# Reordered first loads in a fused attention and two-mixture kernel

## The chip, the cores and the metric

The kernel runs on one core of a Trainium2 chip. Its engines are TensorE (PE, matrix products; PEld is its weight load), VectorE (DVE), ScalarE (ACT), GpSimd (POOL) and SyncE (SP), which here only issues DMAs. The metric is the device time of one execution in microseconds (us), the median of several runs.

## The reference

```python
def _attn_ref(q, k, v):                      # (4, 8, 576, 64): batch, heads, sequence, head size
    q_d = q.reshape(B, H, Sd, 4, D).mean(axis=3)          # the same for k_d and v_d
    out_d = sm_attn(q_d, k_d, v_d)                        # softmax attention of 144 pooled places
    out_up = np.repeat(out_d, 4, axis=2)
    mask = np.abs(pos[:, None] - pos[None, :]) < 4        # band of 7 around each place
    scores = np.where(mask, scale * q @ k.T, -1e9)
    out_local = softmax(scores) @ v
    return out_up + out_local

x = attn_out.transpose(0, 2, 1, 3).reshape(2304, 512)
h = x @ w_in;  x = (h * np.cos(h)) @ w_out                # first mixture, 512 -> 2048 -> 512
xn = x / rms(x) * rms_g                                   # second mixture, 512 -> 1536 -> 512
g = xn @ w_gate;  return (g * sigmoid(g) * (xn @ w_val)) @ w_out2
```

## The kernel before, in words

Everything is one program. A planner (`Order`) writes the order of every engine's instructions ahead of the run: each piece of work is a generator that asks for an engine and a length, for an event, or for a place out of a pool, and the planner hands out turns by earliest start and due time. On the chip each engine then works through its list strictly in that order, and SP issues the DMAs in its own.

The work has three stages. In the first, batch 0 is attended. **Pooled attention**: q and k are loaded in six pieces (tiles `pq`, line 854), summed over four places (`sum4`, q on DVE, k on POOL), transposed (`trq`), multiplied (`sps`), passed through exp (tile `E`), transposed (`tra`) and multiplied with the pooled v (`avp`), which gives `od`. The pooled v come from tiles `v` (lines 475 and 478, 16 loads) and are summed on POOL into `vh` and `vhl` (lines 499 to 506). **Local attention** goes by five blocks `u` of 116 places: q and k of a block are two loads (tile `raw`, line 791), v is four small ones (tile `vb`, line 807, three buffers), then come transposes (`btr`), banded scores (`bs`, which need the band mask `bm`), maximum, exp and normalisation on DVE, ACT and POOL (tile `bE`), a transpose (`bat`), the product with v (`bav`), the sum with `od` on DVE (line 755) and the split into a high and a low part, `big`, on ACT and POOL (lines 768 and 770). The 256 tokens of x tile 0 are complete with the first 24 places of block 2.

The second stage is the first mixture: products `h` (line 1004), h cos h on ACT and DVE, products `y` (line 1070). Its 32 weight pieces (even ones of `w_in`, odd ones of `w_out`, 512 KB each, lines 286 and 288) arrive as 64-bit numbers and are converted in place by `w_conv`: two DVE instructions (lines 311 and 317), two of ACT (315 and 319) and a subtraction on POOL or DVE (line 322). The attention of batches 1 to 3 runs beside it (loads of `pq` at line 431, of `rqk` at 791). The third stage is the second mixture (products `gvp` and `o`).

Memory for the first loads comes out of the 31 places `wa` and `wb` that later hold weights. `start()` takes its places at once; the six of `pq` go into a pool `pqp`, three of which become the tiles `E2` of the blocks' exp, and the other three return when the third `E2` is taken. The list `LOADS` orders the rest of `start()`: "w" stands for weight pieces, "r" for blocks' q and k, "v" for the pooled v. `keep_warm` fills planned gaps of PE with products of the identity (`warm`, line 246) up to the planner's time `FT`.

Of the kernel before, what the change touches and what calls it, by code (L numbers as in the profile page):

```python
# [12 lines left out]
ACTF = mybir.ActivationFunctionType  # L13
# [24 lines left out]
LOADS = (("w", 4), ("r", 1), ("v", 0), ("r", 1), ("w", 4), ("r", 3))  # L38
# [153 lines left out]
def fused_kernel(ctx: ExitStack, tc, q, k, v, w_in, w_out, w_gate, w_val, w_out2, rms_g, mask, bmask, out):  # L192
    nc = tc.nc
    PE, ACT, DVE, POOL, SP = nc.tensor, nc.scalar, nc.vector, nc.gpsimd, nc.sync
    S_ = Order()
# [213 lines left out]
    def pq_first(w, c, t, qs, place):  # L409
# [4 lines left out]
        give("pqp", place)  # L414
# [210 lines left out]
    def block(b, u, raw, pools):  # L625
# [33 lines left out]
        else:  # L659
            if u % 2 == 0:  # L660
                pl = yield take("pqp")
# [173 lines left out]
    def start():  # L835
# [3 lines left out]
        for n in [("pq", w, c) for c in range(3) for w in range(2)] + [("qs", w) for w in range(2)] + [("E", hp) for hp in (1, 2, 3)] \  # L839
                + [("v4", hp) for hp in range(4)] + [("vhl", 0)] + [("raw", u) for u in range(5)]:  # L840
            pl[n] = yield take(PLACES)

# [6 lines left out]
        qs = [early(("qs", w), [128, 9, 64]) for w in range(2)]  # L849
        for c, (u0, n) in enumerate(UC):  # L850
            for w in range(2):
                t = early(("pq", w, c), [128, 4, 4, 64])
                yield "SP", max(0.48, 0.37 * n)
                SP.dma_start(t[:, :n], pq_src(0, w, u0, n))
                done(("pq", w, c))
                S_.add(pq_first(w, c, t, qs[w], pl["pq", w, c]), 0.0, S_.now())
        E = EP + [early(("E", hp), [72, 2, 3, 2, 64]) for hp in (1, 2, 3)]
        for hp in range(4):
            yield "POOL", 0.8
            POOL.memset(E[hp], 0.0)  # L860
        yield take("E")
        for hp in range(4):
            S_.add(pooled(0, hp, E[hp]), 0.0)
        vh0 = early(("vhl", 0), [128, 2, 3, 128])
        vh0 = VH + [vh0[:, 0], vh0[:, 1]]
        for x in vh0:
            yield "POOL", 0.5
            POOL.memset(x, 0.0)
        yield "SP", 0.96, (0, None)
# [3 lines left out]
        yield "ACT", 1.0  # L873

        for x, (d0, d1) in enumerate(((0, 3), (3, 3), (3, 10))):
            for s, d in enumerate((d0, d1)):
                pr = slice(64 * s, 64 * s + 64) if d0 != d1 else slice(0, 128)
                if d0 != d1 or s == 0:
                    ACT.activation(out=bm[pr, x], in_=bf[pr, 16 - d:80 - d], func=ACTF.Copy)
        done("mask")  # L880
# [22 lines left out]

        first = 0
        for what, n in LOADS:
# [3 lines left out]
            elif what == "w":  # L909
                yield from words(n)  # L910
            else:
# [927 lines left out]
```

## Time and profile before

| what | value |
|---|---|
| median of 3 runs | 985.36 us (984.74 to 2394.44) |
| profiled execution, its own time | 986.51 us |
| its span, first to last instruction | 984.7 us |
| mean granted clock of PE | 0.994 |
| PE busy | 954.6 us (97%) |
| DVE busy | 724.0 us (74%) |
| POOL busy | 268.5 us (27%) |
| DMA, loads and stores of the queue | 134.85 MB, 45.4% of 16 engines |

Busy shares are means over the three stages, so they say little about any one of them; what bounds the start is read from stretches of the span. A busy PE includes the `warm` products, which compute nothing.

### The profile page before, as it was taken

What the parts mean: (1) busy time and instruction counts of PE and PEld (TensorE: products, weight loads), DVE (VectorE), ACT (ScalarE), POOL (GpSimd) and SP (SyncE); (2) the same over time, 40 slices, a digit from 0 to 9 for tenths busy, and PEclk for the clock granted to TensorE, in tenths of its full rate; (3) what the DMA queues carried; (4) which work ended last, traced back from release to release, by engine and by line L of the source; (5) the groups of instructions that cost most, each with busy time, mean ns of one, the idle gap of its engine ahead of it and who ended that gap; (6) DMA issues with size and microseconds to landing.
All of it is one profiled execution on the core that took longest, in us unless ns stands there. A gap on an engine that the chain in (4) does not pass through costs nothing.

```text
span 984.7 us, 19115 instructions
## 1 busy us (share of the span) xinstructions
PE 954.6 (97%) x7102; PEld 881.4 (90%) x7102; DVE 724.0 (74%) x1460; ACT 542.8 (55%) x1090; POOL 268.5 (27%) x325
## 2 busy tenths in 40 slices
PE   7788899999999999999999999999999999999998
PEld 7787788888988888888888889999999999999998
DVE  3889976577767675666577599586666688999895
ACT  3657886577676964657566475242322334544442
POOL 3867675444345311000042252000000014300000
PEclk9999999899999999999999999999999999999999
DMA  8788633567675554544331311133222144454432
GB/s 245 211 234 252 179 116 118 140 204 185 201 220 153 173 168 137 167 153 165 124 129 65 107 43 49 49 105 93 75 81 70 57 146 131 137 169 137 143 119 76
DMA packets 160333, 136.07 MB, mean 138 GB/s; under 512 B 72176, under 2 KB 133744, under 8 KB 160240
## 3 DMA queue, kind: packets, MB, share of 16 engines
q1 hardware_dynamic: 160240, 134.85, 45.4%
q8 instruction: 56, 0.92, 0.4%
q14 instruction: 37, 0.30, 0.1%
HBM read 98.64 MB, written 36.18 MB: 137 GB/s over the span
## 4 chain that ended last, share of the span: by engine, by line
PE 83%; POOL 4%; DVE 3%; SPq 3%; issue 3%; DMA 2%; ACT 2%; DVEq 0%; POOLq 0%; ACTq 0%
PE gvp L1493 26%; PE y L1070 19%; PE h L1004 18%; PE o L1746 13%; PE bav L745 2%; PE btr L641 1%; SPq L475 1%; POOL wwa L322 1%; DMA v<-in_v 1%; SPq L807 1%; PE avp L589 1%; PE bs L684 1%; PE yt L1398 1%; PE bat L720 1%; SPq L478 1%
## 5 line engine op out<-in xcount | busy, mean ns | idle before, releaser
L1493 PE MATMUL gvp<-xc,wc 128*128 128x384 f32 x1296 | 231.7, 335 | 0.0
L1493 PEld LDWEIGHTS gvp<-xc,wc 128*128 128x128 f32 x1296 | 225.6, 188 | 0.3
L1564 DVE TENSOR_TENSOR tmp<-gvp,tmp 128x384 f32<-128x384 f32 x180 | 99.3, 553 | 54.6 <-PE gvp L1493 51.4
L1004 PE MATMUL h<-big,wwa 128*128 128x256 f32 (+1 forms) x756 | 126.1, 320 | 1.6 <-DVE t L1029 1.0
L1004 PEld LDWEIGHTS h<-big,wwa 128*128 128x128 f32 x756 | 109.4, 193 | 11.9 <-DVE t L1029 1.2
L1746 PE MATMUL o<-wo,wc 128*128 128x256 f32 x972 | 118.9, 280 | 0.0
L1746 PEld LDWEIGHTS o<-wo,wc 128*128 128x128 f32 x972 | 116.1, 190 | 0.0
L1070 PE MATMUL y<-wwa,big 128*128 128x512 f32 x432 | 109.6, 398 | 1.7 <-DVE big L1040 1.7
L1070 PEld LDWEIGHTS y<-wwa,big 128*128 128x128 f32 x432 | 78.9, 188 | 18.7 <-DVE big L1040 2.7
L1004 PE MATMUL h<-big,wwb 128*128 128x256 f32 (+1 forms) x504 | 85.2, 320 | 0.1
L1070 PE MATMUL y<-wwb,big 128*128 128x512 f32 x324 | 82.3, 399 | 2.3 <-POOL big L1040 2.3
L1024 DVE SCALAR_TENSOR_TENSOR t<-kk,h 128x512 f32<-128x512 int32 x72 | 49.0, 681 | 42.4 <-ACT kk L1022 42.1
L1004 PEld LDWEIGHTS h<-big,wwb 128*128 128x128 f32 x504 | 73.1, 193 | 7.7 <-issue 0.8
L1022 ACT ACTIVATE kk<-h 128x512 int32<-128x512 f32 x72 | 42.7, 593 | 58.4 <-PE h L1004 58.2
L1070 PEld LDWEIGHTS y<-wwb,big 128*128 128x128 f32 x324 | 59.0, 188 | 14.7 <-POOL big L1040 2.9
L1630 POOL TENSOR_TENSOR wt<-wo 128x256 f32<-128x256 f32 x10 | 9.9, 987 | 208.7 <-DVE wc L1349 183.3
L1029 DVE TENSOR_TENSOR t<-h,t 128x512 f32<-128x512 f32 x72 | 49.3, 685 | 18.1 <-ACT t L1027 17.6
L1555 ACT ACTIVATE tmp<-gvp 128x384 f32<-128x384 f32 x36 | 17.7, 492 | 75.9 <-PE gvp L1493 75.9
L1027 ACT ACTIVATE t<-t,cst 128x512 f32<-128x512 f32 x72 | 51.9, 722 | 13.2 <-DVE t L1024 12.7
L1038 ACT ACTIVATE big<-t 128x512 fp32r<-128x512 f32 x72 | 45.2, 629 | 25.0 <-DVE t L1029 23.6
L1689 ACT ACTIVATE wc<-ut 128x512 fp32r<-128x512 f32 (+1 forms) x60 | 34.3, 584 | 43.4 <-DVE ut L1675 27.2
L1040 DVE TENSOR_TENSOR big<-t,big 128x512 fp32r<-128x512 f32 x54 | 40.0, 741 | 16.5 <-ACT big L1038 16.2
(185 smaller groups left out, 1737.8 us busy)
## 6 DMA issues: line engine op xcount, KB each, us to landing
us<-tmp SPq DMA_DIRECT2D x72, 192.0 KB, 2.0
uf<-us SPq DMA_DIRECT2D x48, 256.0 KB, 2.9
rawwa<-in_moe_w_out SPq DMA_DIRECT2D x21, 512.0 KB, 4.5
wfs<-rawwa SPq DMA_DIRECT2D x36, 256.0 KB, 2.3
rawwa<-in_moe_w_gate SPq DMA_DIRECT2D x12, 512.0 KB, 4.0
rawwa<-in_moe_w_val SPq DMA_DIRECT2D x12, 512.0 KB, 4.4
wf<-wfs SPq DMA_DIRECT2D x12, 512.0 KB, 4.1
vb<-in_v SPq DMA_DIRECT2D x80, 64.0 KB, 2.7
```

Source lines behind the costliest of these rows:

```text
L1004: PE.matmul(h[:, w_ * ci:w_ * ci + w_], a[:, ksl], x_at(x, kk), start=m == 0, stop=m == 11)
L1022: ACT.activation(out=kk, in_=h, func=ACTF.Copy, scale=INV2PI, bias=0.25)
L1024: DVE.scalar_tensor_tensor(out=t, in0=kk, scalar=TWOPI, in1=h, op0=ALU.mult, op1=ALU.subtract)
L1027: ACT.activation(out=t, in_=t, func=ACTF.Sin, scale=-1.0, bias=cst[:, 0:1])
L1029: DVE.tensor_tensor(out=t, in0=h, in1=t, op=ALU.mult)
L1038: ACT.activation(out=gh, in_=t, func=ACTF.Copy)
L1040: (POOL if e == "POOL" else DVE).tensor_tensor(out=gl, in0=t, in1=gh, op=ALU.subtract)
L1070: PE.matmul(y[j][b], g[:, tsl], a, start=(first and ci == 0 and i == 0), stop=(last and c == 15 and i == 2))
L1493: PE.matmul(bank, w[:, a, kk], xc[:, x, b, kk], start=first and i == 0, stop=i == 5, skip_group_check=True)
L1564: DVE.tensor_tensor(out=half(o), in0=a, in1=half(b), op=ALU.add)
L1689: ACT.activation(out=o[:, 0], in_=src, func=ACTF.Copy)
L1746: PE.matmul(b[m][1][:, l], u[0][x][:, j, l], w[:, y, k], start=(p == 0 and l == 0 and i == 0), stop=(p == C3 - 1 and i == 2), skip_group_c ...
```

## The change

`LOADS` gets three new letters and `start()` is split so that they can stand anywhere: "m" makes the band mask's copies, "q" loads the six pieces of pooled q and k, "e" clears the tiles of the pooled attention. The new list loads the mask, then q and k of blocks 0 and 1, then the pooled q and k, two weight pieces instead of four, the pooled v, block 2, four weight pieces, and blocks 3 and 4. A place is taken for the first `E2` at the start (`e2p`), so that blocks 0 and 1 need not wait for a pooled place; of the six pooled places the first two that come free serve the other two `E2`, and the other four go back to the weights' pools at once.

```diff
-LOADS = (("w", 4), ("r", 1), ("v", 0), ("r", 1), ("w", 4), ("r", 3))
+FB = 1
+LOADS = (("m", 0), ("r", 2), ("q", 0), ("e", 0), ("w", 2), ("v", 0), ("r", 1), ("w", 4), ("r", 2))
@@ pq_first
-        give("pqp", place)
+        cnt["pqp"] = cnt.get("pqp", 0) + 1
+        give("pqp" if cnt["pqp"] < 4 - (FB > 0) else place[2], place)
@@ block
-                pl = yield take("pqp")
+                pl = yield take("pqp" if u or not FB else "e2p")
@@ start
-                + [("v4", hp) for hp in range(4)] + [("vhl", 0)] + [("raw", u) for u in range(5)]:
+                + [("v4", hp) for hp in range(4)] + [("vhl", 0)] + [("raw", u) for u in range(5)] + [("E2", 0)] * (FB > 0):
             pl[n] = yield take(PLACES)
+        if FB:
+            give("e2p", pl["E2", 0])
...
+        def sums(cs):
+            for c in cs:
+                u0, n = UC[c]
+                for w in range(2):
+                    t = early(("pq", w, c), [128, 4, 4, 64])
+                    yield "SP", max(0.48, 0.37 * n)
+                    SP.dma_start(t[:, :n], pq_src(0, w, u0, n))
+                    done(("pq", w, c))
+                    S_.add(pq_first(w, c, t, qs[w], pl["pq", w, c]), 0.0, S_.now())
...
+        def pool0():
+            for hp in range(4):
+                yield "POOL", 0.8
+                POOL.memset(E[hp], 0.0)
...
+            for x in vh0:
+                yield "POOL", 0.5
+                POOL.memset(x, 0.0)
...
+            elif what == "q":
+                yield from sums(range(3))
+            elif what == "m":
+                S_.add(masks(), -10.0)
+            elif what == "e":
+                S_.add(pool0(), -10.0)
...
-        yield wait(("E2", 2))
-        for _ in range(3):
-            p = yield take("pqp")
-            give(p[2], p)
```

The order of all engines through much of the first mixture is planned anew by this; PE's lists agree again in their last 180 of some 665 rows. Three places matter for the prediction. In the fences a number behind a tile's name tells tiles of one name apart; line numbers of the changed kernel are 1 or 2 higher for the same work, and its pooled loads stand at line 887.

**SP, the start of its queue.** First before: pooled q and k (`pq`), v of blocks 0 to 2 (`vb`), the mask (`bf`), four weight pieces (`rawwb`), block 0 (`raw0`).

```order
L854 DMA pq00_109<-in_q 128x1024
L807 DMA vb_98<-in_v 64x4x64 x4
L854 DMA pq10_111<-in_k 128x1024
L807 DMA vb_99<-in_v 64x4x64 x4
L854 DMA pq01_117<-in_q 128x1024
L807 DMA vb_100<-in_v 64x4x64 x4
L854 DMA pq11_140<-in_k 128x1024
L854 DMA pq02_167<-in_q 128x256
L854 DMA pq12_183<-in_k 128x256
L872 DMA bf_259<-band_mask 64x144 x2
L286 DMA rawwb2_267<-in_moe_w_in 128x4x256
L288 DMA rawwb3_281<-in_moe_w_out 128x1024
```

Now, from the queue's first load on:

```order
L856 DMA bf_107<-band_mask 64x144 x2
L809 DMA vb_98<-in_v 64x4x64 x4
L793 DMA raw0_116<-in_q 128x8x64
L809 DMA vb_99<-in_v 64x4x64 x4
L793 DMA raw0_116<-in_k 128x8x64
L809 DMA vb_100<-in_v 64x4x64 x4
L793 DMA raw1_132<-in_q 128x8x64
L793 DMA raw1_132<-in_k 128x8x64
L887 DMA pq00_168<-in_q 128x1024
L887 DMA pq10_171<-in_k 128x1024
L887 DMA pq01_186<-in_q 128x1024
L887 DMA pq11_216<-in_k 128x1024
```

Four loads of local q and k moved ahead of the pooled ones; two weight pieces fell from the stretch ahead of the pooled v, whose 16 loads follow in both.

**SP, behind the pooled v.** Before: block 1 stands first here, block 2 behind four weight pieces, blocks 3 and 4 behind the v of block 3 (`vb_98`).

```order
L286 DMA rawwb8_525<-in_moe_w_in 128x4x256
L288 DMA rawwb9_573<-in_moe_w_out 128x1024
L791 DMA raw2_576<-in_q 128x8x64
L431 DMA pq_599<-in_q 128x512
L791 DMA raw2_576<-in_k 128x8x64
L431 DMA pq_625<-in_q 128x512
L807 DMA vb_98<-in_v 64x4x64 x4
L791 DMA raw3_624<-in_q 128x8x64
L791 DMA raw3_624<-in_k 128x8x64
```

Now, from block 2 on:

```order
L793 DMA raw2_433<-in_q 128x8x64
L793 DMA raw2_433<-in_k 128x8x64
L287 DMA rawwb5_446<-in_moe_w_in 128x4x256
L289 DMA rawwb6_473<-in_moe_w_out 128x1024
L287 DMA rawwb7_506<-in_moe_w_in 128x4x256
L289 DMA rawwb8_533<-in_moe_w_out 128x1024
L793 DMA raw3_535<-in_q 128x8x64
L793 DMA raw3_535<-in_k 128x8x64
L793 DMA raw4_586<-in_q 128x8x64
L793 DMA raw4_586<-in_k 128x8x64
L932 DMA cst_86<-in_moe2_rms_g 128x4x1
L433 DMA pq_617<-in_q 128x512
```

Block 2 now comes straight behind the pooled v and blocks 3 and 4 ahead of the `vb` that waits; the seventh and eighth weight pieces (`rawwb8_525`, `rawwb9_573` before) stand behind that `vb` now, and from the ninth piece on the two queues have it at the same or nearly the same place.

**POOL, from the end of the pooled v's sums.** Before:

```order
L506 TENSOR_TENSOR vhl0_235<-v43_394 48x64
L322 TENSOR_TENSOR wwa12_441<-rawwb4_286,wwa12_441 128x512
L322 TENSOR_TENSOR wwa17_522<-rawwb6_460,wwa17_522 128x512
L322 TENSOR_TENSOR wwa13_502<-rawwb5_293,wwa13_502 128x512
L375 TENSOR_TENSOR pq_599<-pq_599 128x2x128
L770 TENSOR_TENSOR big_93<-bt_627,big_93 128x4x116
L377 TENSOR_TENSOR qs_598<-pq_599 128x128
L375 TENSOR_TENSOR pq_625<-pq_625 128x2x128
L322 TENSOR_TENSOR wwa14_560<-rawwb7_482,wwa14_560 128x512
L377 TENSOR_TENSOR qs_598<-pq_625 128x128
L770 TENSOR_TENSOR big_93<-bt_742,big_93 128x4x116
```

Now (`big_93` three times: blocks 0 and 1, then the 24 places of block 2 that complete x tile 0):

```order
L323 TENSOR_TENSOR wwa17_332<-rawwb4_289,wwa17_332 128x512
L323 TENSOR_TENSOR wwa2_513<-rawwb5_446,wwa2_513 128x512
L323 TENSOR_TENSOR wwa4_583<-rawwb7_506,wwa4_583 128x512
L323 TENSOR_TENSOR wwa3_545<-rawwb6_473,wwa3_545 128x512
L376 TENSOR_TENSOR pq_617<-pq_617 128x2x128
L772 TENSOR_TENSOR big_93<-bt_640,big_93 128x4x116
L378 TENSOR_TENSOR qs_616<-pq_617 128x128
L772 TENSOR_TENSOR big_93<-bt_664,big_93 128x4x116
L376 TENSOR_TENSOR pq_657<-pq_657 128x2x128
L378 TENSOR_TENSOR qs_616<-pq_657 128x128
L323 TENSOR_TENSOR wwa5_596<-rawwb8_533,wwa5_596 128x512
L772 TENSOR_TENSOR big_93<-bt_785,big_93 128x4x24
```

Block 1's part follows block 0's after one instruction instead of four, and block 2's after three more; before, seven stood between the second and the third.

Counted over whole lists: `warm` products fall from 112 to 82, but 24 of them stand behind the first `h` now, against 4. Ahead of the first h cos h step (`t<-kk,h`) DVE has 8 instructions of line 312 and 7 of line 318 in the changed kernel, against 12 and 10 of the same two conversion steps (lines 311 and 317) before.

## Rows read from the trace of the kernel before

**Rows 1.** The page, part 1: busy us (share of span) xinstructions.

```profile
PE 954.6 (97%) x7102; PEld 881.4 (90%) x7102; DVE 724.0 (74%) x1460; ACT 542.8 (55%) x1090; POOL 268.5 (27%) x325
```

**Rows 2.** Busy time by stretch: width, engines (xinstructions), PE clock, DMA share, GB/s.

```profile
0.00:60.00 60.00, 48.04 (x536) 44.29 (x537) 36.28 (x68) 32.06 (x91) 38.62 (x58) 1.00 0.82 220
60.00:100.00 40.00, 35.82 (x374) 31.48 (x374) 37.47 (x62) 28.17 (x51) 29.81 (x31) 1.00 0.86 255
100.00:130.00 30.00, 26.62 (x202) 23.04 (x201) 28.44 (x55) 26.73 (x54) 18.63 (x22) 0.94 0.59 169
150.00:598.00 448.00, 442.51 (x3264) 383.83 (x3263) 308.45 (x619) 293.46 (x566) 138.16 (x173) 0.99 0.47 145
```

**Rows 3.** Timeline of PE: start us, us, instruction, [idle before <-releaser].

```profile
46.02 1.14 PE L745 MATMUL bav<-bt,vb 64*64 64x58 f32 x32
47.10 2.27 PE L246 MATMUL warm<-ident 128*128 128x128 f32 x18
...
64.33 1.14 PE L745 MATMUL bav<-bt,vb 64*64 64x58 f32 x32
...
67.76 1.73 PE L1004 MATMUL h<-big,wwa 128*128 128x256 f32 x12
...
106.16 1.54 PE L534 MATMUL sps<-pqs 64*72 64x144 f32 x8 [2.66 <-DVE bst L704]
...
171.25 1.96 PE L745 MATMUL bav<-bt,vb 64*64 64x58 f32 x30 [1.64 <-DVE bt L755]
```

**Rows 4.** Timeline of POOL, pooled v to x tile 0.

```profile
20.42 0.78 POOL L868 MEMSET vh<- 128x384 f32 x2
...
27.12 0.73 POOL L499 TENSOR_TENSOR v<-v 128x256 f32<-128x256 f32 x1 [5.20 <-DMA v<-in_v]
...
45.16 4.08 POOL L322 TENSOR_TENSOR wwa<-rawwb,wwa 128x512 fp32r<-128x512 f32 x3
49.21 0.72 POOL L375 TENSOR_TENSOR pq<-pq 128x256 f32<-128x256 f32 x1
49.89 1.61 POOL L770 TENSOR_TENSOR big<-bt,big 128x464 fp32r<-128x464 f32 x1
...
67.27 0.58 POOL L770 TENSOR_TENSOR big<-bt,big 128x96 fp32r<-128x96 f32 x1 [0.27 <-ACT big L768]
```

**Rows 5.** Timeline of SP's DMA issues: start us, us.

```profile
18.52 4.16 SPq L475 DMA_DIRECT2D v<-in_v  x1
...
40.45 0.43 SPq L791 DMA_DIRECT2D raw<-in_k  x1
...
47.08 2.73 SPq L807 DMA_DIRECT2D vb<-in_v  x4
...
60.46 0.42 SPq L286 DMA_DIRECT2D rawwb<-in_moe_w_in  x1
```

**Rows 6.** Busy time by stretch again: small rows (4 to 12 us), weight pieces (16 to 20).

```profile
4.00:12.00 8.00, 6.27 (x36) 5.87 (x35) 2.47 (x2) 0.82 (x2) 1.99 (x2) 1.00 0.93 227
16.00:20.00 4.00, 3.41 (x28) 3.11 (x28) 0.14 (x1) 1.39 (x4) 4.00 (x8) 1.00 1.05 352
```

**Rows 7.** Waits of SP's queue, 0 to 80 us: total us, times, longest.

```profile
SPq L431 <- POOL qs L377: 4.9, 4, 1.7
```

**Rows 8.** Timeline of DVE: start us, us.

```profile
29.80 0.99 DVE L555 TENSOR_TENSOR E<-E,stat 72x288 f32<-72x288 f32 x2
...
44.23 0.68 DVE L317 SCALAR_TENSOR_TENSOR rawwb<-rawwb 128x512 int32<-128x512 int32 x1
...
45.16 0.41 DVE L311 TENSOR_SCALAR rawwb<-rawwb 128x512 int32<-128x512 int32 x1
...
47.27 1.31 DVE L755 TENSOR_TENSOR bt<-bav,od 64x464 f32<-64x464 f32 x2 [1.69 <-PE bav L745]
```

**Rows 9.** Busy time by stretch, the two at a lowered PE clock.

```profile
106.00:110.00 4.00, 3.84 (x20) 3.44 (x21) 4.00 (x9) 3.93 (x6) 1.75 (x3) 0.57 0.81 224
171.30:178.50 7.20, 7.20 (x57) 7.07 (x58) 2.53 (x4) 1.70 (x5) 5.67 (x8) 0.54 0.52 111
```

More of the change, by code (lines that the diff above doesn't have):

```diff
@@ L847, in load @@
             yield "SP", us
[L849 to L869, printed above, removed]
+        yield "SP", 0.96
         bf = wb.tile([128, 144], F32, tag=f"wb{NB - 1}", name="bf")
@@ L872, in start @@
             SP.dma_start(bf[64 * s:64 * s + 64], bmask[0:64])
[L873 to L880, printed above, removed]
+        qs = [early(("qs", w), [128, 9, 64]) for w in range(2)]
         def values0():
@@ L902, in raws, with masks @@
                 S_.add(block(0, u, (t[:, 0], t[:, 1]), (None, (pl["raw", u][2], pl["raw", u]))), blk_due(0, u))
+        def sums(cs):
[7 more added lines that the diff above has]
+                    S_.add(pq_first(w, c, t, qs[w], pl["pq", w, c]), 0.0, S_.now())
+        def masks():
+            yield "ACT", 1.0
+            for x, (d0, d1) in enumerate(((0, 3), (3, 3), (3, 10))):
+                for s, d in enumerate((d0, d1)):
+                    pr = slice(64 * s, 64 * s + 64) if d0 != d1 else slice(0, 128)
+                    if d0 != d1 or s == 0:
+                        ACT.activation(out=bm[pr, x], in_=bf[pr, 16 - d:80 - d], func=ACTF.Copy)
+            done("mask")
+        E = EP + [early(("E", hp), [72, 2, 3, 2, 64]) for hp in (1, 2, 3)]
+        vh0 = early(("vhl", 0), [128, 2, 3, 128])
+        vh0 = VH + [vh0[:, 0], vh0[:, 1]]
+        def pool0():
+            for hp in range(4):
+                yield "POOL", 0.8
+                POOL.memset(E[hp], 0.0)
+            yield take("E")
+            for hp in range(4):
+                S_.add(pooled(0, hp, E[hp]), 0.0)
+            for x in vh0:
+                yield "POOL", 0.5
+                POOL.memset(x, 0.0)
         first = 0
```

## The prediction, made before the changed kernel ran

> **What bounds the kernel now.** I read the page first, then the span by stretches, then the timelines of PE, POOL, SP and DVE up to the first product of the mixture, then the waits. The page says that PE is busy 97% of the span [rows 1]; the stretches say where that holds. From 150 to 598 us PE is busy 442.5 of 448 us, and from there to the end it runs on alone, so behind 150 us a saving counts only as far as PE can start its work sooner. Up to 60 us PE's 48.0 busy us are mostly the warming products. DVE is the engine to look at in between: 36.3 of the first 60 us, but 37.5 of the next 40 and 28.4 of the 30 after those, that is 65.9 of 70 us [rows 2]. So there are three regimes: a start limited by loads and by chains of small steps, a stretch from 60 to 130 us in which DVE is full with weight conversions, h cos h and attention, and a long rest in which PE is full.
>
> The first h starts at 67.76 us [rows 3]. The chain ahead of it: the pooled v arrive, POOL begins to sum them at 27.12 and has the last at 45.16 [rows 4]; the products bav of blocks 0 and 1 follow at 46.02 [rows 3]. Block 2, needed for x tile 0, comes late: its k is issued at 40.45, behind four weight pieces [rows 5], and its bav runs at 64.33, its low part on POOL at 67.27 [rows 3, 4]. SP stands still ahead of the v of block 3, which waits for the bav of block 0 and goes out at 47.08 [rows 5]; blocks 3 and 4 are queued behind it.
>
> **Part 1, bytes ahead of the pooled v.** Before: six pooled pieces (2304 KB), twelve vb (768), mask (72), four weight pieces (2048), block 0 (512): 5704 KB. Now two weight pieces less and one block more: 5192 KB. The rows of q, k and vb are 256 bytes long, and the stretch with most of them moved 227 GB/s at a busy share of 0.93, while the one with weight pieces moved 352 at a full share [rows 6]. Taking off 1024 KB at 352 saves 3.0 us, adding 512 KB at 227 costs 2.3: net -0.7; at one rate for both (255 GB/s, the mean from 60 to 100 us [rows 2]) it would be -2.0. I take -1. The 16 loads of v themselves are paced by SP's issue in both.
>
> The Trainium skill, "DMA: Bandwidth & Descriptors", section "Why small descriptors are slow (HBM only)", puts a 256-byte descriptor at 11 cycles where 8 carry data, 27% lost, which speaks against loading blocks first; rows 6 agree, 244 against 335 GB/s for a full share. By the page's loss at the 352 of the weight pieces the added block would cost 2.0 us and the term be -1.0, inside what I have.
>
> **Part 2, POOL's sums of v.** They took 18.0 us, from 27.12 to 45.16 [rows 4], with two weight subtractions among them; now one stands there (-1.4, a third of the 4.08 us for three), but three of the four clearings of vh come between the sums instead of before them (+1.2, each half of 0.78). So they end about -0.2 from the sums themselves and -1 from part 1 sooner: about 44.0. The pooled scores start later, since pooled q and k are behind four loads (1024 KB, 4.5 us at 227 GB/s), but the last of their exp tiles was normalised on DVE by 30.8 [rows 8], and the last vh was summed only at 45.16; that slack covers it. If it doesn't, up to 4.5 us come back here; that is an end of the range.
>
> **Part 3, block 2 and the first h.** Block 2's loads now come straight behind v, some 6 us sooner, and its scores no longer wait. Behind 44.0: bav of two blocks by 45.6, four additions of od at half of 1.31 each on DVE by 48.2, block 2's normalisation with one conversion between (four steps, which I estimate at the 0.68 of line 317: 2.7) by 50.9 [rows 8]; transpose, copy and bav of block 2, 0.7 + 0.6 + 1.1, by 53.3; two more additions, 54.6. POOL's own list is longer: four weight subtractions (4 x 1.36), the sum of pq (0.72), big of block 0 (1.61), qs (smaller than pq's sum, 0.5), big of block 1 (1.61), pq and qs (1.2), a subtraction (1.36), the 24 places (0.58): 13.0 us behind 44.0 gives 57.0 [rows 4]. So the first h moves from 67.8 to about 57, **-11 us**. Blocks 3 and 4 no longer stand behind the waiting vb.
>
> **Part 4, what comes back while DVE is full.** The 11 us reach the end only if DVE follows. It idled 23.7 us of the first 60 [rows 2]. Blocks 0 and 1 fill a part of it, but DVE now begins with block 0's scores, later than it did with the first pooled sum; I put its idle time up to the same point at 19 to 24 us, so it is 0 to 5 us ahead. Beside that, four first steps (0.41) and three second steps (0.68) of the conversions stand behind the first h cos h instead of ahead of it: 3.7 us that come sooner for h but are owed to the weights that follow [rows 8]. The weights also limit it: the ninth piece, issued at 60.46 before, has the same place in SP's list; now it goes behind vb of block 2, whose bav ends about 53.3, plus four issues (2.73 for four [rows 5]): some 57, 3 to 4 us sooner, not 11. DVE and the weights so agree on a lead of 3 to 6 us; of the 11 I give back **+5** (bounds 0 and +11).
>
> **Part 5, warming products.** Twenty more stand behind the first h. Nine (18 instructions) took 2.27 us, so one is 0.25 us [rows 3] and twenty are 5.0 if the gap for which each was planned is not there, nothing where it is. PE idled in the stretch 60 to 130 for 7.6 us [rows 2], which is a place for most of them; I take **+1**. The thirty fewer in all lie in front of the first h, where PE is not the bound: 0.
>
> **Part 6, places.** In the first 80 us the longest of the queue's waits is that of the pooled loads (line 431) for a ring place, 4.9 us [rows 7]; a weight load (line 286) that waits for a place isn't in that view. Giving four places back sooner, and holding one more for E2, is worth 0; at the most as much as those 4.9 us would shift.
>
> Sum: -11 + 5 + 1 = **-5 us** on the profiled execution's 986.51, or 981.5; the median was 985.36, 1.15 less, so I forecast a median of **980.4**.
>
> **Rivals.** *The whole shift reaches the end.* If DVE's order, with conversions put behind h cos h, keeps PE fed, PE is 11 us ahead for good: 975 to 974. For it: PE had only 7.6 us of idle from 60 to 130 [rows 2]. Against it: DVE's 65.9 of 70 us, and the ninth piece's 3 to 4 us.
>
> *Nothing is left.* PE starts h sooner, runs out of converted weights after the first three h groups (the seventh piece now stands behind the vb of block 3 that waits for bav, and stood ahead of it) and meets the old schedule at 100 us: 985. For it: DVE's total work is the same, and in this regime it alone sets the pace. Against it: DVE has idle time to gain.
>
> *Slower: PE starves and its clock falls.* The place is 60 to 130 us, behind the first h groups. PE's wait of 2.66 us ahead of 106.16 was followed by a stretch at 0.57 of the clock, that of 1.64 ahead of 171.25 by one at 0.54 [rows 3, 9]; the two stretches of 4.0 and 7.2 us cost about half of that at full clock, 1.7 and 3.3 us. PE would be started 11 us sooner into a stretch in which less weight is ready; each hole would cost about 2.2 us of idle time and 2.5 of slow clock, 4.7. With one such hole and the warming products at +1 the time is that of before; it decides from the second on: three of them (14), the warming products at full price (5) and the gain of part 1 to 4 (-6) give +13, 998; for 2% (1005) there would have to be five. The rule that the clock is one of two steps, full when PE has been busy and half after it has idled, is in the Trainium skill, "TensorE: Matmul & The Clock Gate", section "What's actually happening". By that rule the trace agrees: the granted values lie between 1.2 GHz and 2.4 GHz only because the stretches in rows 9 are cut a little wider.
>
> *The change doesn't do what it says:* v of the pooled attention, not block 2, holds everything, and if POOL is later by the 4.5 us of part 2 the first h moves by 6 only and the rest is eaten by part 4: 985, as with "nothing".
>
> **How the numbers follow.** Forecast (977 to 983) 0.45, the whole shift 0.18, nothing left (983.5 to 987, with the last rival) 0.21, slower 0.16. The range takes the forecast, most of the whole shift and nothing-left, and the first hole or two of the slower case: 972 to 992. A reordering of the whole plan adds a scatter of a few us that no row prices. Two per cent is 19.7 us, about what a measurement of this kernel can tell from no change: faster by it would need a shift of twice the 11 us, 0.03; slower by it five holes, 0.04; within it 0.93.
>
> **What would show it.** Right: first h near 57 us, the last sum of the pooled v on POOL near 44, DVE's idle time of the first 60 us at 19 or less with more than 95% busy from 57 to 120, PE's idle from 57 to 130 larger than the 7.6 us of 60 to 130 now, and the second mixture's first gvp some 5 us sooner. Wrong: first h later than 62 (part 2 or 3), or low-clock stretches beyond the two of before (the slower rival), or a PE that is full from 57 us on (the whole shift).

## The result and the profile after

The changed kernel takes 992.97 us (median of 6, 990.35 to 994.13), the kernel before 984.55 beside it: ratio 1.0083, 95% interval [1.0071, 1.0096]. That is 8.4 us slower: the time moved the other way from the forecast of 980.4 and lies 1 us above its range. One of the six executions of the kernel before took 2394.44 us; the ratio goes by fast executions alone and leaves it out. The profiled execution took 993.51 us (span 991.7, granted clock 0.984).

First the stretches of the changed kernel, in the columns of [rows 2]:

```profile
0.00:60.00 60.00, 40.83 (x451) 36.49 (x452) 41.00 (x75) 30.65 (x87) 36.02 (x56) 0.88 0.77 209
60.00:100.00 40.00, 38.06 (x395) 34.45 (x394) 33.07 (x55) 31.27 (x54) 27.07 (x27) 0.96 0.82 240
100.00:130.00 30.00, 25.49 (x205) 22.09 (x204) 24.39 (x41) 23.04 (x42) 21.38 (x20) 0.89 0.55 158
150.00:598.00 448.00, 441.58 (x3259) 381.33 (x3260) 303.08 (x596) 297.96 (x573) 143.66 (x184) 0.99 0.47 147
```

DVE, the third pair, is busier in the first 60 us (41.0, before 36.3), as forecast, but then no longer full: 57.5 of the 70 us from 60 to 130, where it had 65.9 [rows 2]. It is full just behind that, from 130 to 150 us, where the kernel before had it 14.0 us busy. First before, then changed:

```profile
130.00:150.00 20.00, 18.62 (x162) 16.07 (x161) 14.04 (x29) 16.53 (x31) 17.36 (x21) 1.00 0.40 125
```

```profile
130.00:150.00 20.00, 16.39 (x122) 14.38 (x121) 19.86 (x33) 15.31 (x30) 18.44 (x20) 1.00 0.48 152
```

PE's granted clock is below 1 in each of the first three stretches (0.88, 0.96 and 0.89).

PE around the first h, to be read beside [rows 3] (the name has moved to L1018):

```profile
47.30 2.08 PE L747 MATMUL bav<-bt,vb 64*64 64x58 f32 x64
...
58.09 1.08 PE L722 MATMUL bat<-ident,bE 128*128 128x128 f32 x4 [3.83 <-DVE bE L708]
...
60.81 1.97 PE L747 MATMUL bav<-bt,vb 64*64 64x58 f32 x32
...
65.10 1.68 PE L1018 MATMUL h<-big,wwa 128*128 128x256 f32 x12
```

The first h is at 65.10 us: 2.7 sooner than 67.76, not 11. POOL's first sum of pooled k is at 19.16, of pooled v at 28.59, and its last sum of v ends at 46.39 (beside [rows 4]):

```profile
19.16 1.27 POOL L376 TENSOR_TENSOR pq<-pq 128x512 f32<-128x512 f32 x1 [17.82 <-DMA pq<-in_k]
...
28.59 0.72 POOL L501 TENSOR_TENSOR v<-v 128x256 f32<-128x256 f32 x1 [0.51 <-DMA v<-in_v]
...
45.62 0.77 POOL L508 TENSOR_TENSOR vhl<-v 48x64 f32<-48x64 f32 x1
```

DVE between bav of blocks 0 and 1 and that of block 2 (beside [rows 8]; L312 and L318 are the first and second step of a weight conversion):

```profile
45.33 0.88 DVE L318 SCALAR_TENSOR_TENSOR rawwb<-rawwb 128x512 int32<-128x512 int32 x1 [0.41 <-ACT rawwb L316]
...
46.93 1.20 DVE L312 TENSOR_SCALAR rawwb<-rawwb 128x512 int32<-128x512 int32 x1
...
48.70 1.12 DVE L318 SCALAR_TENSOR_TENSOR rawwb<-rawwb 128x512 int32<-128x512 int32 x1
...
50.68 2.64 DVE L757 TENSOR_TENSOR bt<-bav,od 64x464 f32<-64x464 f32 x4
53.35 0.69 DVE L703 TENSOR_REDUCE bst<-bE 128x8 f32<-128x512 f32 x1
...
55.60 1.22 DVE L312 TENSOR_SCALAR rawwb<-rawwb 128x512 int32<-128x512 int32 x1
56.74 1.21 DVE L708 TENSOR_TENSOR bE<-bE,bst 128x512 f32<-128x512 f32 x1
...
62.81 1.31 DVE L757 TENSOR_TENSOR bt<-bav,od 64x464 f32<-64x464 f32 x2 [2.69 <-PE bav L747]
```

And SP's weight loads: the third piece, the seventh, the ninth and the twelfth (beside [rows 5], where the ninth is at 60.46):

```profile
35.28 0.79 SPq L287 DMA_DIRECT2D rawwb<-in_moe_w_in  x1
...
56.29 0.59 SPq L287 DMA_DIRECT2D rawwb<-in_moe_w_in  x1
...
65.31 0.60 SPq L287 DMA_DIRECT2D rawwb<-in_moe_w_in  x1
...
77.56 0.59 SPq L289 DMA_DIRECT2D rawwa<-in_moe_w_out  x1
```

Where the time went is read from two windows, first h to last `yt` of the first mixture, here of the kernel before, then of the changed one:

```profile
67.80:597.90 530.10, 517.15 (x3893) 448.64 (x3893) 381.45 (x745) 360.38 (x693) 197.81 (x238) 0.99 0.50 152
```

```profile
65.10:605.40 540.30, 522.77 (x3940) 453.58 (x3936) 384.97 (x742) 370.56 (x704) 211.97 (x250) 0.99 0.50 153
```

This stretch takes 10.2 us longer. PE's idle time grows from 12.95 to 17.53 us (+4.6), its busy time by 5.6, of which warming products are 5.2 (48 instructions for 6.5 us here, 10 for 1.3 before). With the first h 2.7 us sooner that is +7.5, against +7.0 in the span. Behind the last `yt` the two run alike (386.3 and 386.8 us).

What PE waits for in these windows is in the view of its waits (us in total, times, longest), before and changed, longest first:

```profile
PE sps L534 <- DVE bst L704: 2.7, 1, 2.7
PE y L1070 <- POOL big L1040: 2.3, 2, 1.2
PE y L1070 <- DVE big L1040: 1.7, 2, 1.2
PE bav L745 <- DVE bt L755: 1.6, 1, 1.6
```

```profile
PE bat L722 <- DVE pqs L399: 3.3, 1, 3.3
PE sps L536 <- ACT at L579: 3.2, 1, 3.2
PE y L1084 <- POOL big L1054: 3.1, 2, 2.6
PE y L1084 <- ACT big L1052: 1.6, 1, 1.6
PE bat L722 <- DVE bt L697: 1.2, 1, 1.2
```

Products of the attention that runs beside the mixture (`bat`, `sps`, `tra`, `bav` and the like) account for 9.5 of the 17.5 us, where they had 6.3 of 12.9; the rest is mostly `y` waiting for h cos h (`big`). No wait in either view is put down to the conversion of a weight piece.

### The profile page after: what moved, and what is told of

Read it like the earlier page. It is cut to its first block, busy times and chain, and to the rows that moved or that the text cites. A ratio compares the mean times of both kernels' runs of the same rounds, so it can differ in the third digit from the quotient of the medians.

```text
span 991.7 us, 18990 instructions
## 1 busy us (share of the span) xinstructions
PE 951.3 (96%) x7042; PEld 877.0 (88%) x7042; DVE 727.2 (73%) x1452; ACT 550.3 (55%) x1096; POOL 275.3 (28%) x331
## 4 chain that ended last, share of the span: by engine, by line
PE 82%; DVE 9%; DMA 3%; ACT 3%; SPq 1%; issue 1%; POOL 0%; DVEq 0%; ACTq 0%; POOLq 0%
PE gvp L1507 26%; PE y L1084 17%; PE h L1018 17%; PE o L1760 13%; PE bav L747 2%; PE btr L643 1%; PE avp L591 1%; PE sps L536 1%; PE bs L686 1%; DVE rawwa L312 1%; SPq L809 1%; PE bat L722 1%; DVE rawwa L318 1%; PE yt L1412 1%; PE tra L572 1%
## 5 line engine op out<-in xcount | busy, mean ns | idle before, releaser
L1018 PE MATMUL h<-big,wwa 128*128 128x256 f32 (+1 forms) x756 | 124.8, 316 | 1.1 <-DVE t L1043 1.1
L1018 PEld LDWEIGHTS h<-big,wwa 128*128 128x128 f32 x756 | 108.2, 190 | 11.6 <-DVE t L1043 1.4
L1084 PE MATMUL y<-wwb,big 128*128 128x512 f32 x324 | 84.5, 405 | 4.4 <-POOL big L1054 2.6
L1018 PE MATMUL h<-big,wwb 128*128 128x256 f32 (+1 forms) x504 | 85.4, 322 | 0.0
L1018 PEld LDWEIGHTS h<-big,wwb 128*128 128x128 f32 x504 | 74.0, 196 | 7.1 <-issue 0.9
L1084 PEld LDWEIGHTS y<-wwb,big 128*128 128x128 f32 x324 | 60.2, 192 | 17.7 <-POOL big L1054 3.1
L1054 POOL TENSOR_TENSOR big<-t,big 128x512 fp32r<-128x512 f32 x20 | 29.1, 1455 | 110.7 <-ACT big L1052 104.1
L1052 ACT ACTIVATE big<-t 128x512 fp32r<-128x512 f32 x72 | 45.1, 628 | 23.5 <-DVE t L1043 22.7
```

The costliest lines, as they stand in the source:

```text
L1018: PE.matmul(h[:, w_ * ci:w_ * ci + w_], a[:, ksl], x_at(x, kk), start=m == 0, stop=m == 11)
L1052: ACT.activation(out=gh, in_=t, func=ACTF.Copy)
L1054: (POOL if e == "POOL" else DVE).tensor_tensor(out=gl, in0=t, in1=gh, op=ALU.subtract)
L1084: PE.matmul(y[j][b], g[:, tsl], a, start=(first and ci == 0 and i == 0), stop=(last and c == 15 and i == 2))
```

## The experiments

Every kernel was timed beside the kernel before; ratios below are to that. Each profile is of one execution, which for some kernels is slower than their median (e1 997.73 us for 995.11, e6 1002.2 for 997.40). Four moments or sums of each profile are set beside the ratio: the first h, when SP sends the twelfth weight piece, when the subtraction of the 24th converted piece ends, and PE's idle time between the first h and the last `yt`.

| kernel | ratio [95%] | first h | 12th sent | 24th ready | PE idle |
|---|---|---|---|---|---|
| before | 1 | 67.8 | 63.8 | 130.7 | 12.9 |
| changed | 1.0083 [1.0071, 1.0096] | 65.1 | 77.6 | 140.2 | 17.5 |
| e1 | 1.0096 [1.0063, 1.0128] | 66.9 | 78.4 | 141.3 | 21.1 |
| e2 | 1.0174 [1.0150, 1.0198] | 67.4 | 73.6 | 147.2 | 18.0 |
| e3 | 1.0070 [1.0054, 1.0087] | 60.8 | 78.4 | 145.1 | 21.4 |
| e4 | 1.0007 [0.9991, 1.0023] | 71.1 | 63.1 | 131.1 | 13.0 |
| e5 | 1.0143 [1.0102, 1.0184] | 67.3 | 69.9 | 140.8 | 21.0 |
| e6 | 1.0110 [1.0072, 1.0149] | 70.5 | 71.3 | 145.2 | 22.7 |
| e7 | 1.0198 [1.0169, 1.0227] | 66.4 | 78.6 | 141.9 | 21.5 |
| e8 | 1.0081 [1.0056, 1.0107] | 70.6 | 64.5 | 128.8 | 16.0 |
| e9 | 1.0086 [1.0061, 1.0111] | 69.2 | 81.8 | 144.3 | 16.6 |
| e10 | 1.0221 [1.0204, 1.0239] | 75.8 | 87.0 | 154.7 | 23.8 |
| e11 | 1.0107 [1.0088, 1.0126] | 68.2 | 84.5 | 143.0 | 20.9 |
| e12 | 1.0139 [1.0124, 1.0154] | 66.0 | 85.0 | 145.3 | 18.7 |
| e13 | 1.0126 [1.0106, 1.0145] | 66.0 | 70.4 | 144.7 | 18.9 |
| e14 | 1.0081 [1.0061, 1.0102] | 66.7 | 70.9 | 141.6 | 14.5 |
| e15 | 1.0171 [1.0154, 1.0188] | 67.2 | 66.6 | 140.1 | 20.8 |
| e16 | 1.0171 [1.0148, 1.0194] | 60.6 | 71.1 | 142.3 | 23.3 |
| e17 | 1.0156 [1.0139, 1.0174] | 68.2 | 70.3 | 139.4 | 19.2 |
| e18 | 1.0138 [1.0109, 1.0167] | 60.6 | 64.0 | 136.9 | 22.3 |

**Which part: e4 and e12.** e4 has the old order of the loads with the new places, e12 the new loads without the places. e4 is not quite the places alone: it keeps the new code of `start()`, so the band mask is loaded first and SP's steps no longer come after POOL's clearing.

```diff
+LOADS = (("q",0),("e",0),("m",0),("w",4),("r",1),("v",0),("r",1),("w",4),("r",3))   # e4
-FB = 1
+FB = 0                                                                              # e12
```

> The changed kernel with the loads in their old order (pooled q and k, mask, four weight pieces, block 0, v, block 1, four pieces, three blocks), so of the change only the places that are given back sooner are left. If the order of the loads carries the loss: 983 to 987, first h at 67 to 68, 4 warming products behind it. If the places alone carry it (their use reorders the plan behind 60 us): 990 to 994. If any new plan scatters by several us whatever the loads: anything from 980 to 992, with the first h where it was.

> The changed kernel without its places (no place given back sooner, none held for E2), so the new loads alone. The old loads with the new places gave 984.9, so if the two parts are separate the new loads alone carry the loss: 990 to 996, 24th piece at 138 or later. If it takes both: 984 to 988.

e4: 984.91 us, no difference. e12: 999.14, above the 990 to 996 that was expected. So the places cost nothing with the old loads, and the loss came with the new ones. (With the new loads the kernel that has the places is 6 us faster, which is less than a new plan alone moves, e7 below.) That the order of the loads carries the loss is the nearest reading, but not shown by this pair: both are new plans too, and a new plan alone moved the time by 8.5 and 11.5 us (e7, e8). e4 also says something of the first h: it comes at 71.14, the latest but one of the table, and the kernel is as fast as before.

**The warming products: e1.**

```diff
-FT = 90
+FT = 55
```

> The changed kernel with warming products planned only up to 55 us: the 24 behind the first h are gone, the other instructions keep their order. Theory W (warming products planned into gaps that are not there push PE's work back): PE's 5.2 us of them behind the first h go, 988 us, PE's idle time behind the first h stays near 17.5 us. Theory I (they stand in gaps that are there anyway, since PE waits for DVE and the weights): the idle time grows by about 5 us in their place, 992 to 993. Theory C (they keep the clock up): the half-clock stretches behind 65 us, 13.6 us long in the changed kernel, get longer, 994 or more.

995.11 us, no faster. Theory W falls: the 48 instructions are gone, but in the profiled execution (997.73 us) PE's idle time behind the first h is 21.1 us instead of 17.5, and its busy time hardly falls:

```profile
66.90:609.70 542.80, 521.66 (x3896) 450.26 (x3889) 383.20 (x741) 370.20 (x704) 210.54 (x250) 0.98 0.50 152
```

Theory I has part of it and C the rest: stretches at half clock (1.2 of 2.4 GHz) behind the first h sum to 20.5 us instead of 13.7, and executions lie between 987.89 and 998.64. So most of the warming products stood in gaps that are there anyway: without them the gaps show as idle time and as more of the lower clock.

**The start: e3.** Pooled q and k ahead of the two blocks.

```diff
+LOADS = (("m",0),("q",0),("r",2),("e",0),("w",2),("v",0),("r",1),("w",4),("r",2))
```

> The changed kernel with the pooled q and k loaded ahead of the two blocks instead of behind them. Theory P: the pooled scores are back at their old time (first sps product near 21 instead of 29.8 us), POOL starts on the pooled v sooner, the first h comes at 58 to 61 instead of 65.1 us and the time falls by 4 to 7 us, 986 to 989. Theory L (weights 7 to 9 decide, wherever the first h is): first h sooner, but the time stays within 990 to 994, since the ninth piece still waits behind the v of blocks 3 and 4.

The first h comes at 60.76 us, 7 sooner than before, and the time is 992.42, not distinguishable from the changed kernel. Theory P was right about the first h and wrong about the time; L's number came out. A first h that is sooner does not make the kernel faster here.

**The planner's time: e9, e10, e11.** The old `start()` had a pause in it: its SP steps behind the pooled loads came after POOL's clearing in the same generator. In the new code the loads run on without it.

```diff
             else:
+                yield "SP", 0.0, (28.0, None)      # e9; e10: 33.0; e11: 31.0 with e3's LOADS
                 yield from values0()
```

> The changed kernel with one more line: the planner may not place the loads of the pooled v before 28 us of its own time (it placed them from 19.8 on; the chip sent them from 17.8 to 34.0). The order of the loads in the list stays, only what the planner orders around and behind them changes; by its own figures the first h is then at 60.6 instead of 52.3 us (65.1 on the chip in the changed kernel; 71.0 by its figures and 67.8 on the chip in the kernel before). Theory T (the new loading code took out the pause that had kept the planner's time behind the chip's, so every order behind it is made for loads that have not come yet): the 24th converted piece is ready by 135 instead of 140.2 us and the time falls to 982 to 989. Theory L without T (these loads in this order bring the weights late, whatever the planner thinks): 24th piece at 139 or later, 990 to 996.

> The same with 33 us: by the planner's figures the first h is at 68.2, nearly as in the kernel before. Theory T: like the run with 28 us or better, 982 to 988, 24th piece by 135. Theory L without T: 990 to 996. Theory R (any new plan falls some us either way): the two pauses differ by 5 us or more from each other.

> Pooled q and k ahead of the two blocks, which gave the soonest first h so far (60.8 us), and the pooled v not before 31 us of the planner's time. Theory T: first h at 60 to 63 and the pace of the kernel before behind it, 978 to 985. Theory L without T: 24th piece later than 138, 990 to 995, whatever the first h.

993.96, 1007.19 and 996.80 us: theory T falls, as it does by e4, which lacks the pause too and is as fast as before. Planning the pooled v later only made the pieces later (the 24th at 143.0 to 154.7). The two pauses of e9 and e10 differ by 13.2 us, more than the 5 that theory R asked for.

**Two pieces, from both sides: e2, e5, e6, e17, e18.** The old list sends eight pieces by 36.7 us, the new one six by 37.8 and the seventh at 56.29, behind the v that wait for bav.

```diff
+LOADS = (... ("w", 2), ("v", 0), ("r", 1), ("w", 6), ("r", 2))     # e2; e17 with NRAW = 7
+LOADS = (... ("w", 4), ("v", 0), ("r", 1), ("w", 4), ("r", 2))     # e5
+LOADS = (("w",4),("r",1),("v",0),("r",1),("w",2),("r",3))          # e6, in the kernel before
+LOADS = (e3's with ("w", 6)); NRAW = 7                             # e18
```

> The changed kernel with six weight pieces instead of four between block 2 and the last two blocks, so eight pieces stand ahead of the loads that wait for bav of blocks 0 and 1, as in the kernel before. Theory L (weights 7 to 9 come late and DVE's conversions behind them leave PE without work between 85 and 160 us): the ninth piece goes out near 58 instead of 65.3 us, PE's idle time behind the first h falls from 17.5 to 13 or less, 985 to 988. Theory P (the gain was lost ahead of the first h, in the pooled scores that came late): first h still near 65, time 991 to 994. Theory W: 31 warming products stand behind the first h, so 1 to 2 us more than the changed kernel, 994.

> The changed kernel with four weight pieces instead of two ahead of the pooled v: eight pieces ahead of the last two blocks, as in the kernel before, and 1024 KB more ahead of v. Theory L (the supply of converted weights sets PE's pace from 85 to 160 us; the twentieth converted piece is ready at 128.3 us in the changed kernel and at 116.8 in the kernel before): pieces 7 to 12 are sent sooner than the 56 to 78 us of the changed kernel, the twentieth is ready at 118 to 122 and the time falls to 985 to 989. If only the first h counts: v come about 3 us later, first h at 68, 995 or more. Rival R (each new plan falls anywhere within some us): no relation between the twentieth piece and the time.

> The kernel before with two weight pieces less in front of blocks 2 to 4 (two instead of four), everything else as it was: block 2's q and k go out sooner, the seventh and eighth piece stand behind the v that wait for bav, which is that part of the change alone. Theory L: the seventh to ninth piece go out 5 us or more later than the 35 to 60 us of the kernel before, the twentieth converted piece is ready 5 to 10 us later, and the time grows by 4 to 8 us, to 989 to 993, although block 2 is sooner. My forecast's mechanism (first h sooner is what counts): first h at 62 or sooner and 980 to 983. Rival R: anywhere, without relation to the twentieth piece.

> The changed kernel with six pieces instead of four between block 2 and the last two blocks, and seven instead of five pieces that may be loaded and not yet converted, so that all eight go out by 40 us, ahead of everything that waits for a product (in the run with six pieces and the old five the eighth went out at 55 us and the ninth at 69). Theory E (eight pieces early, converted while DVE is still idle, are what the old list has and each slower one lacks): the eighth piece is converted by 69 us, the twelfth by 88 and the 24th by 134; 984 to 990 us. Theory D (in the new order DVE spends that time on the blocks' and the pooled scores, so pieces sent early only lie there): eighth piece at 70 or earlier but the 24th at 139 or later, 991 to 1001.

> The same with pooled q and k ahead of the two blocks. Theory E: first h at 60 to 64 us, 24th piece by 134, 978 to 986. Theory D: 24th piece at 139 or later, 991 to 1001, whatever the first h.

e6 moves two pieces behind the blocks in the kernel before, and nothing else in the list; the rest is planned anew. It takes 997.40 us, outside what theory L gave for it (989 to 993). The seventh piece goes out at 52.65 (35.20 before), the 24th is ready 14.5 us later:

```profile
52.65 0.60 SPq L286 DMA_DIRECT2D rawwb<-in_moe_w_in  x1
...
142.58 1.32 POOL L322 TENSOR_TENSOR wwb<-rawwa,wwb 128x512 fp32r<-128x512 f32 x1
143.86 1.31 POOL L322 TENSOR_TENSOR wwa<-rawwa,wwa 128x512 fp32r<-128x512 f32 x1
```

(The 24th ends with the second of these, at 145.2; at 130.7 in the kernel before.) Block 2's bav did not gain by it either: first h at 70.5, not 62. So the forecast's first step, that sending block 2's loads sooner brings the first h sooner, falls here in a single edit.

From the changed side the repair failed each time. In e2 the eighth piece went out only at 55.0 and the ninth at 69.3, so it did not test what it was made for; its 1002.57 us lie above every range given for it. In e5 the twentieth converted piece was ready at 115.2 us, sooner than the 116.8 of the kernel before, and it took 999.05 us where theory L had 985 to 989. e17 sent eight pieces by 38.1 us, and yet the 24th was ready at 139.4 and the time was 999.56 us. e18 has everything that I had asked for, first h at 60.65 and sixteen pieces sent by 66.7 us,

```profile
60.65 2.52 PE L1018 MATMUL h<-big,wwa 128*128 128x256 f32 x19
```

```profile
66.65 2.00 SPq L289 DMA_DIRECT2D rawwa<-in_moe_w_out  x1
```

with DVE busy 66.2 of the 70 us from 60 to 130, and the 24th piece is still at 136.9, PE's idle time 22.3 us and the time 997.38. Theory E falls. D's numbers for the 24th piece and the time came out for e17 (its eighth piece was converted at 72.6 us, not by 70), and e18's 24th piece lies between the two.

**Sending 9 to 16 sooner: e13 to e16.** A condition in the planner puts pieces ahead of batch 1's loads.

```diff
         yield wait("late")
+        yield wait(("wl", 1, 13))       # set where piece 14's load is issued; e14: 15
         for b in range(1, B):
...
+                if (b, u) == (1, 0):    # in block_v; e15 with e5's LOADS, e16 with e3's
+                    yield wait(("wl", 1, 13))
                 x = yield take("vb")
```

> The changed kernel with one condition in the planner: the loads of batch 1's blocks (q, k and v) may not be put on the list before the fourteenth weight piece. So pieces 12 to 14 no longer stand behind loads that wait for products. Theory L: the twelfth piece goes out at 68 to 70 instead of 77.6 us, the 24th converted piece is ready by 135 instead of 140.2, and the mixture ends (last yt product) at 598 to 601 instead of 605.4; 985 to 989 us. Theory D (DVE is the limit; late pieces only follow from what it does first): pieces sent sooner wait longer for their first step on DVE, 24th piece at 138 or later, 991 to 997.

> The same up to the sixteenth piece. Theory L: as with fourteen or 1 to 2 us better, 984 to 988, unless batch 1's blocks then come late for x tile 2, which would show as PE waiting for big behind 130 us. Theory D: 991 to 997.

> Four pieces ahead of the pooled v (999.1 us without the condition) and pieces 9 to 14 ahead of batch 1's loads. Theory L: the twelfth piece goes out below 70 us, the 24th is ready by 135, 986 to 992, 7 us or more better than without the condition. Theory D: 996 to 1001, no relation.

> Pooled q and k ahead of the two blocks (first h at 60.8 us, 992.4 without the condition) and pieces 7 to 14 ahead of batch 1's loads. Theory L: the twelfth piece goes out at 66 to 70 instead of 78.4 us, 24th piece by 136, and since the first h is 7 us sooner than in the kernel before, 979 to 986. Theory D: 991 to 996.

996.63, 992.50, 1001.16 and 1001.96 us. The twelfth piece does go out at 66.6 to 71.1 us, and the 24th is ready at 140.1 to 144.7 all the same. Theory L in its simple form (send sooner, be ready sooner) falls; D's ranges held for e13 and e14, while e16 is 6 us above its range. e14 shows what takes its place: with sixteen pieces in front, DVE has less to do from 100 to 130 (18.8 us busy, 24.4 in the changed kernel), and the work of the blocks on it moves behind 130 (instructions that write `bst`, `bE` or `bt` and begin from 130 to 160 take 8.9 us, 4.1 in the changed kernel).

**Planning anew: e7 and e8.** The same loads, with another figure for a load's landing in the planner.

```diff
-    DMALAT = 2.0
+    DMALAT = 2.05
```

> The changed kernel with the planner's figure for a load's landing at 2.05 instead of 2.0 us: the first products of PE keep their order, buffers and places are given out differently, and what follows is planned anew with the same loads. Rival R (the 8 us are an accident of one plan): the time moves by 4 us or more, down to 985 or up to 1000. Theory L (it is in the first loads): 990 to 995, the twentieth piece again at 125 to 131 us.

> The kernel before with the same figure at 2.05 instead of 2.0 us, so a plan made anew with the old loads. Rival R: moves by 4 us or more, to 989 or above or 981 or below. Theory L: 982 to 988, twentieth piece ready at 114 to 120 us.

1004.45 and 992.86 us: 11.5 us more than the changed kernel, 8.5 more than the kernel before, for nothing that any row of the start would price. Rival R is right about the size. But the two lose in different places. In e8 the 24th piece is ready at 128.8, sooner than before, and the kernel is slower all the same; it loses between 400 and 500 us, where PE waits for `big`:

```profile
448.60 0.49 PE L1070 MATMUL y<-wwb,big 128*128 128x512 f32 x1 [1.68 <-ACT big L1038]
450.00 2.80 PE L1070 MATMUL y<-wwb,big 128*128 128x512 f32 x11 [0.91 <-POOL big L1040]
```

From 400 to 500 us PE is busy 95.16 us in e8 and 99.65 in the kernel before. e7 has the changed kernel's late pieces (141.9) and loses more on top.

## Why the prediction was wrong

**The sign's cause.** Two steps failed. Part 3 put the first h at 57 us and the gain at 11 us; the gain was 2.7. And the sum took a lead of the first h for a lead of PE's end, less 5 and 1 us (parts 4 and 5); behind the first h 10.2 us were lost. In the terms of the sum, forecast -11 + 5 + 1 = -5 against -2.7 + 10.2 = +7.5, part 3 was short by 8.3 us and parts 4 and 5 together by 4.2. The second step is the deeper one, for where part 3's aim was reached, in e3, e16 and e18 (first h at 60.6 to 60.8), the time was 992 to 1002 us, and e4, with the first h at 71.1, took 985. Over the twenty kernels of the table the first h says nothing of the profiled span (correlation 0.11). PE's idle time behind it (0.82) and the 24th converted piece (0.73) go with the span, but less so among the seventeen kernels that do not have the old loads (0.64 and 0.47), and PE's idle time is itself a part of the span.

The three kernels that have the old loads (before, e4, e8) have the 24th piece at 128.8 to 131.1, all seventeen others at 136.9 or later. An early 24th piece is a sign of the old loads, then, and not shown to be the cause of their time: e8 has the earliest and takes 992.86 us, and no weight piece stands in the two views of PE's waits above.

The forecast's own signs of being wrong came: the first h later than 62, and low-clock stretches beyond the two. The second mixture's first gvp, forecast some 5 us sooner, came at 584.4 us instead of 576.9, 7.5 later.

**Part 1** (-1 us): POOL's first sum of v is 1.5 us later, not sooner; SP began the sixteen v sooner but spread them further, from 17.77 to 33.38, where it had been 18.52 to 31.92. Bytes alone did not tell it.

**Part 2** (sums of v end at 44.0): 46.39. The slack for the pooled scores held, in the sense that POOL's last sum still ended behind DVE's last normalisation of E (43.8); but those normalisations now lie at 37.1 to 43.8, where conversions had stood.

**Part 3** (-11 us): from bav of blocks 0 and 1 (47.30) to that of block 2 (62.78) I had 44.5 to 53.3. DVE first did conversion steps and block 2's own scores, which I had taken as done, so the sums with `od` began at 50.68; block 2's normalisation took from 53.35 to 57.95, 4.6 us instead of four times 0.68, since single instructions were stretched to 1.21 and 1.22; and bat and bav ran at half clock, 1.08 and 1.97 us where they take 0.60 and 1.14 at 68.48 and 70.69. The POOL list that I thought longer was not what decided: ahead of the low part of the 24 places POOL idled 1.9 us for ACT.

**Part 4** (+5, bounds 0 and 11): the ninth piece, forecast at 57, was sent at 65.31, behind batch 1's v that wait for block 2's bav, and DVE was not over 95% busy from 57 to 120 us but 86% (54.1 of 63 us). Parts 4 and 5 together were 10.2 us, of a lead that was 2.7. That DVE and the supply of weights would set the lead is not what the runs show: DVE was less busy than before, and PE's waits were for the attention and for h cos h.

**Part 5** (+1, bounds 0 and 5): 5.2 us of PE's time, but without them e1 was no faster. **Part 6** (0): right with the old loads (e4).

**The rivals.** The slower one, at 0.16, named what came: holes for PE behind the first h and a falling clock. Idle time grew by 4.6 us, and half-clock stretches behind the first h by 3.4: there are three, of 6.8, 3.4 and 3.4 us at 117.5, 151.6 and 175.5, where there were two of 3.4 and 6.8 (rows 9 cuts them wider). Each begins within 1.2 us of the end of a wait of PE: 3.33 us up to 117.03, 3.21 up to 150.48, 1.60 up to 174.93. Its sum of +13 was for three more holes, and one half-clock stretch more came; its reason, that less weight is ready, is not in PE's waits.

```profile
117.50:124.30 6.80, 6.77 (x32) 5.81 (x31) 4.93 (x11) 5.60 (x12) 4.17 (x2) 0.50 0.21 76
```

Its place, 60 to 130, was somewhat too early: counted in PE's instructions other than the warming ones, the changed kernel is 3.0 us ahead at 84 us and 0.5 at 103, and 2.8 behind at 125 and 8.0 at 158.

**What stays open.** Shown is where the time went: idle time of PE behind the first h, more of it at half clock, and warming products in gaps. Shown too is that a sooner first h (e3), no warming products (e1), pieces sent sooner (e5 and e13 to e18) and a later plan for the pooled v (e9 to e11) do not bring the time back, and that the places cost nothing with the old loads (e4). That the order of the loads is the cause is likely, since no kernel with a changed order was under 992.4 us, but it is not shown: a plan made anew from the same loads lies 8.5 to 11.5 us higher (e7, e8), and e8, with the old loads, takes 992.86. So part or all of the 8.4 us may be no property of these loads, but of leaving one plan that was better than its neighbours; against that, e4's plan is new as well and cost nothing. Which move of the order would do it is open too. The one remark on "a scatter of a few us that no row prices" was too small by a factor of two to three, and should have widened the range upwards and taken chance from "faster". No experiment separates the two shares, and no version beat the kernel before.

## What to carry to other kernels

Where an engine's lists are written by a planner, price the change only after pricing a plan made anew without it: here that alone was 8.5 us with the old loads and 11.5 with the new, as much as the largest term of the sum. The first product of a stage is a poor goal when other engines feed the stage: list what the stage's own engine waits for behind that product (here the attention beside it and h cos h, and in neither profile a weight piece), and ask of each load that is moved ahead which loads now queue behind a wait. Warming products in gaps aren't cheap or dear by themselves; taking them out only showed the gaps.

## What the runs showed of the hardware

DVE's first conversion step takes 0.41 us alone [rows 8], but up to 3.33 us beside POOL. The case, DVE first, then POOL:

```profile
144.67 0.68 DVE L1043 TENSOR_TENSOR t<-h,t 128x512 f32<-128x512 f32 x1
145.27 3.33 DVE L312 TENSOR_SCALAR rawwa<-rawwa 128x512 int32<-128x512 int32 x1
148.52 0.68 DVE L1038 SCALAR_TENSOR_TENSOR t<-kk,h 128x512 f32<-128x512 int32 x1
```

```profile
144.64 2.58 POOL L323 TENSOR_TENSOR wwa<-rawwa,wwa 128x512 fp32r<-128x512 f32 x2
147.18 0.72 POOL L501 TENSOR_TENSOR v<-v 128x256 f32<-128x256 f32 x1
147.85 0.46 POOL L503 TENSOR_TENSOR v<-v 128x128 f32<-128x128 f32 x1
```

It starts while POOL subtracts and gets through only as the fourth POOL instruction ends at 148.31, while the neighbours that read the product tile h keep their 0.68. The Trainium skill, "SBUF — State Buffer", section "Who interferes with whom", says that tensor_scalar can enter a mode in which it contends with GpSimd, that an instruction with two inputs in SBUF contends with a GpSimd instruction that reads SBUF, and that whoever issues first has the shared ports for its whole instruction while the other fully blocks. The trace agrees on which instructions are hit: of those that begin in the first 160 us, line 312 takes 0.98 us in the mean where POOL is busy at its start and 0.42 where it is not, line 318 0.98 and 0.68, line 557 0.83 and 0.45, line 708 0.90 and 0.69, while lines 1038 (0.67) and 695 (0.41 and 0.42) do not change. But here the wait went over four of POOL's instructions in a row, not one. In the first 160 us the first conversion steps sum to 25.8 us for 29 in the changed kernel and 21.0 for 30 before:

```profile
L312 DVE TENSOR_SCALAR rawwa<-rawwa 128x512 int32<-128x512 int32 x17 | 16.6, 989 | 0.7 <-DMA rawwa<-in_moe_w_in 0.7
L312 DVE TENSOR_SCALAR rawwb<-rawwb 128x512 int32<-128x512 int32 x12 | 9.2, 771 | 0.0
```

These sums do not follow the time: e4, as fast as before, has 23.3 us for 31, and e2, at 1002.57 us, 20.4 for 29.

What a lower clock of PE early on costs, these runs do not show: e4 runs at half clock from 56.9 to 60.2 and from 80.8 to 84.1 us (granted 0.50 in both), where the kernel before does not, and ends level with it; but it has none of the two stretches at 106 and 171 us that the kernel before has [rows 9].
